# New issue orders and engine choices in both attention layers of a four-layer kernel

## The chip, the cores and the metric

The kernel runs on one core of a Trainium2 chip. The metric is the device time of one execution in microseconds (us). The core has five engines that run side by side, each taking its own instructions strictly in the order in which they were issued to it: TensorE (PE, matmuls and transposes), VectorE (DVE), ScalarE (ACT), GpSimd (POOL) and SyncE (SP, which here only issues DMAs). DMAs can be issued from SP's queue, ACT's or POOL's. An instruction waits on semaphores for the results that it needs, and whatever was issued behind it on the same engine waits with it.

## The reference, cut to what matters

A sequence of 2048 positions with 512 features goes through four layers, alternating between a convolution layer A and an attention layer B. Each adds its result to its input; the input is layer-normalised.

```python
def _A_ref(u, A_re, A_im, B_re, B_im, C_re, C_im, log_dt, Dskip):
    ...  # S4: build a 2048-tap kernel per channel, long convolution, + u * Dskip

def _B_ref(x, wqkv, wo):
    H = 32; Dh = D // H
    W, dil = 8, 2
    qkv = (x @ wqkv).reshape(B, S, 3, H, Dh) ...
    idx = pos[:, None] - (jnp.arange(W) * dil)[None, :]
    mask = idx >= 0
    ...
    logits = jnp.einsum("bhsd,bhswd->bhsw", q, kg) * scale
    logits = jnp.where(mask, logits, -1e9)
    attn = _softmax(logits, axis=-1)
    o = jnp.einsum("bhsw,bhswd->bhsd", attn, vg)
    return o.reshape(B, S, D) @ wo
```

So in an attention layer every position of each of the 32 heads (16 features each) looks at itself and at seven earlier positions, two apart.

## The kernel before, in words

**Stages.** The convolution kernel and the first convolution fill the span to about 160 us, attention 1 runs to about 272, convolution 2 (`a_layer`) to about 320, attention 2 to the end. `b_layer` (L1253) builds both attention layers. X holds the residual stream in bf16, 16 column blocks j of 128 positions each; position p*16+j lies on partition p, so that "two positions earlier" is mostly block j-2 on the same partition.

**An attention layer.** Work is named by fp (head group of 16 heads, 0 or 1) and jh (half of the 16 blocks).

- *Turned input.* X is transposed in four quarters q and two feature halves cp into U (XT in the code), by a transposing DMA from SP (L1307) or by eight PE transposes into pt_x (L1301) and a copy by ACT or DVE (L1304).
- *Statistics* for the normalisation: `BATCH_NORM_STATS2` on DVE in halves of 256 features (L1359) or whole (L199), aggregates (L1363), then logarithm and exponential on ACT (L1374, L1375), which give rs. The products of two rs per tap make RR (L1406 on DVE, spread by ACT at L1386, first rows set by POOL).
- *Queries and keys.* Four 128x512 matmuls make a tile ps_qk; `pair` (L1439, evacuated at L1444) takes two tiles in one or two PSUM tiles, `proj` (L1420, evacuated at L1425) takes one. ACT or DVE casts the tile into qT or kT. The last key columns are copied ahead of the first ("ahead", L1462) by DMA, ACT or DVE.
- *Logits.* DVE multiplies queries and shifted keys (prod, L1519, four instructions of 4096 elements for each fp and jh, or eight of 2048 for the first), PE sums over the features of a head with a block matrix (Lp, L1530), a cast LT (L1548) and a turn (pt_l, L1556) bring them to L (L1561).
- *Softmax.* DVE scales by RR (L1599), takes a tree of maxima (L1580) and subtracts (L1644), ACT takes the exponential (L1645); for one group PE subtracts (L1654) and ACT reads PSUM (L1658). The sum is taken on PE (ps_den, L1636) with logarithm and exponential on ACT, or by a tree and a reciprocal on DVE (L1611). DVE multiplies by it (L1664).
- *Values.* PE makes ps_v (L1474), ACT scales it into VX (L1485); SP's DMAs shift parts of VX by one partition (L1498). DVE multiplies values and weights (prod, L1695), PE sums the eight taps with an identity into po (L1711; L1716 in the form with small matmuls that needs no turn afterwards), ACT casts po to ot (L1729) or straight to oT (L1731); ot is turned by a DMA (L1734) or by PE and ACT (L1741, L1744). The last four blocks of head group 1 go in two small pieces, 12 and 14.
- *Output.* PE multiplies oT by wo into ps_o (L1795). X is then updated in one of four ways: the PE adds X itself first (L1792) and ACT casts back (L1905, L1907); DVE adds (L1767); ACT takes the result (L1773) and DVE adds it (L1776); or ACT takes it and a DMA from POOL adds it to X in memory (L1779).
- *After it.* Attention 1 normalises the new X into U for convolution 2 (squares L1913, norms on ACT L1917 or DVE L228); attention 2 stores X to the output (L1942) from SP's or ACT's queue.

**Buffers.** The products (prod) share a ring of four buffers; PSUM has two tiles psA, two psO and one psL. A tile is handed on when its last reader is done.

**What sets the order.** Nothing is scheduled at run time. `Plan` (L314) numbers the operations as they are built. Where an operation can be done in several ways, `either` builds all of them and each has numbers of its own. `run` (L340) then goes through the stage's string of numbers in `ORDERS` (L247) and issues those operations in that order; a way whose numbers aren't in the string is dropped. So a string fixes both the order on each engine's queue and the engine of each choice. The microseconds in the code (`pl.op("A", 0.71, ...)`) aren't used by `run`.

```python
        order = [int(i) for i in ORDERS[Plan.turn].split()]
        Plan.turn += 1
        taken = {self.ops[i][2] for i in order}
        ...
        for i in order:
            fn, after, way = self.ops[i]
            assert done.issuperset(after)
            fn()
            done.add(i)
```

There are four strings: the first convolution, attention 1, convolution 2, attention 2.

Of the kernel before, what the change touches and what calls it, by code (L numbers as in the profile page):

```python
# [230 lines left out]
def load_params(nc, pp, prm):  # L231
# [16 lines left out]
    "164 1 162 236 3 7 8 9 2 5 19 24 20 166 10 12 13 21 11 22 34 14 25 35 30 31 26 28 55 47 45 48 168 56 59 38 42 39 57 62 "  # L248
    "60 43 233 71 65 235 69 66 49 160 72 75 232 81 83 84 87 76 234 229 91 89 73 95 365 323 92 101 85 368 107 103 327 369 "
    "108 96 328 158 174 176 170 370 104 113 329 93 117 371 330 184 172 186 115 180 331 326 116 238 125 105 372 131 127 182 "  # L250
    "373 128 367 178 144 332 341 139 242 188 137 119 245 244 249 382 342 141 140 239 343 189 143 120 344 191 151 190 129 "
    "192 383 246 152 193 194 345 384 346 195 243 149 333 385 202 334 196 132 206 374 216 250 251 230 252 335 375 336 376 "
    "377 200 337 222 268 378 262 338 379 339 380 277 267 198 263 226 208 269 347 340 348 349 351 386 387 270 275 381 388 "
    "264 353 214 278 483 354 356 274 484 204 279 389 237 390 392 394 395 530 240 225 210 221 284 241 358 276 219 213 282 "
    "529 532 533 359 487 285 280 546 283 281 314 397 361 489 488 485 286 534 315 318 535 536 304 486 547 319 537 362 548 "
    "296 297 538 527 399 402 549 490 539 300 550 400 403 291 292 540 509 541 301 302 405 406 309 519 520 310 322 551 542 "
    "409 410 407 408 411 552 412 543 421 514 515 414 523 440 553 544 415 418 554 429 545 294 555 556 419 560 441 442 561 "
    "491 445 446 524 426 321 443 444 558 563 469 427 453 428 571 572 576 577 711 714 665 669 447 574 579 666 671 672 670 "
    "713 565 568 667 566 434 500 668 715 716 496 569 435 581 582 454 455 728 505 584 585 717 311 718 506 719 729 709 720 "
    "470 461 420 721 471 673 497 730 587 588 722 731 593 594 589 498 590 723 591 734 724 592 462 463 596 597 691 507 678 "  # L260
    "679 619 480 481 696 604 697 600 601 725 735 612 613 616 605 847 851 726 732 617 727 853 733 736 737 738 742 848 743 "
    "516 740 854 892 627 643 436 849 850 895 910 602 700 618 852 896 624 698 625 897 898 753 754 899 900 746 608 609 682 "
    "901 902 756 477 747 911 912 913 914 882 478 628 903 915 748 904 905 906 758 759 629 761 705 750 763 706 644 751 764 "
    "958 907 635 766 767 645 626 908 909 525 651 610 887 769 775 888 770 776 771 772 773 774 873 878 652 879 916 960 975 "
    "778 779 917 653 976 977 978 979 891 636 687 782 637 918 922 961 962 963 964 965 688 923 783 785 790 980 680 920 809 "
    "966 925 981 791 659 660 801 967 793 662 689 817 927 792 930 928 931 810 663 811 968 969 933 934 798 939 940 799 937 "
    "938 970 971 818 819 935 972 973 864 806 807 869 936 974 982 708 870 784 833 983 987 988 986 990 855 860 861 825 941 "
    "834 949 992 995 994 808 997 840 826 830 831 998 999 1000 890 872 800 863 1001 946 947 1002 1003 948 1004 841 1005 "
    "1009 1014 1010 1022 842 954 955 1011 881 1012 1038 844 1023 845 1019 956 1013 1030 1039 1020 1040 1025 1046 1031 1047 "
    "1037 1026 1048 1063 1064 1054 1060 1061 1057 1021 1055 1058",  # L270
    "127 169 126 168 40 170 83 172 175 145 173 146 136 132 102 262 304 305 84 128 171 263 264 93 214 259 103 46 260 261 "
    "215 85 7 216 131 273 325 326 44 86 50 43 190 87 253 13 196 197 198 0 235 236 237 56 129 1 199 39 200 201 191 82 192 "
    "45 254 255 174 176 316 317 2 322 283 238 239 89 125 88 90 91 42 41 47 222 130 133 177 392 240 393 394 395 284 398 399 "
    "396 48 134 178 179 323 397 402 406 181 229 230 182 403 231 400 401 407 404 405 408 285 298 299 313 314 307 295 296 "
    "292 293 331 332 289 290 410 411 412 183 424 416 417 352 353 286 287 413 319 320 418 419 414 415 346 420 334 347 343 "
    "344 425 426 427 428 340 358 480 341 359 349 350 381 382 484 485 429 422 423 486 355 356 482 430 481 459 460 461 462 "
# [26 lines left out]
    "843 853 580 581 572 573 806 813 570 587 571 595 588 589 590 601 596 786 597 602 598 584 586 593 776 854 594 599 600 "  # L303
    "591 729 592 603 811 917 809 730 735 925 731 732 741 742 926 918 919 739 844 740 939 733 734 831 736 743 744 927 737 "
    "738 883 884 920 745 746 893 894 863 747 864 940 941 953 954 955 873 874 857 969 859 861 807 907 967 909 904 971 974 "
    "905",
]


# [1668 lines left out]
```

## Time and profile before

| what | value |
|---|---|
| time, median of 3 runs | 430.04 us (429.09 to 430.61) |
| span of the profiled execution | 429.5 us |
| PE busy | 379.0 us |
| VectorE busy | 402.9 us |
| ScalarE busy | 321.2 us |
| GpSimd busy | 27.7 us |

The profile is of one execution, whose span is 0.5 us under the median of the runs. Rows of its timeline read: start, duration, engine, line, operation, output and inputs with their shapes, how many in a row, and in brackets how long the engine had stood idle before and what ended that. Durations of single PE instructions contain their latency, so that rows of several overlap. A row of a window table gives for a stretch of time the busy time of each engine, then the granted PE clock as a share of full speed, and the DMA engines' load.

### The profile page before, as it was taken

The page shows a single profiled execution, that of the slowest core. Times are in us where ns is not written, and L with a number is a line of the kernel's source. Part 1 is how long each engine was busy: PE and PEld are TensorE (multiplying, and loading weights), DVE is VectorE, ACT ScalarE, POOL GpSimd, SP SyncE. Part 2 cuts the span into 40 slices and gives each one's busy share as a digit, 9 for nine tenths or more (in the row PEclk, how much of TensorE's full clock was granted, in tenths as well). Part 3 has the DMA queues.
Part 4 walks back from the last instruction along what each step waited for, and adds up shares of the span by engine and source line. Part 5 has one row for each costly group of instructions (what it writes and reads, how often), then busy time and mean ns, then how long its engine had stood idle before and what let it go on. Part 6 is the DMA issues. An engine that isn't in the chain of part 4 may idle for free.

```text
span 429.5 us, 11615 instructions
## 1 busy us (share of the span) xinstructions
PE 379.0 (88%) x4834; PEld 235.4 (55%) x4834; DVE 402.9 (94%) x682; ACT 321.2 (75%) x524; POOL 27.7 (6%) x97
## 2 busy tenths in 40 slices
PE   2269868997998889999997899899999999998996
PEld 1153646776877764347643345577864336743452
DVE  6999999899999789999899989999889899999995
ACT  7999999999998664668752478999956578853341
POOL 1000000000000200000000510020000010000150
PEclk9757989999999999999999799999999999999999
DMA  8997067688977774012222597099973000222297
GB/s 231 201 294 292 37 87 150 150 161 173 187 123 140 143 173 102 0 38 60 77 55 56 123 209 159 14 178 191 188 121 28 37 2 2 86 85 56 44 154 189
DMA packets 102203, 51.49 MB, mean 120 GB/s; under 512 B 81851, under 2 KB 94028, under 8 KB 101894
## 3 DMA queue, kind: packets, MB, share of 16 engines
q1 hardware_dynamic: 98214, 44.98, 48.9%
q0 software_dynamic: 3104, 5.24, 6.4%
q8 instruction: 38, 0.62, 0.6%
q10 hardware_dynamic: 832, 0.52, 0.4%
q14 instruction: 15, 0.12, 0.1%
HBM read 19.30 MB, written 6.29 MB: 60 GB/s over the span
## 4 chain that ended last, share of the span: by engine, by line
PE 46%; DVE 23%; ACT 9%; issue 4%; DMA 1%; DVEq 0%; ACTq 0%
PE po L1711 8%; PE ps_v L1474 7%; PE ps_qk L1420 6%; PE ps_qk L1439 6%; DVE prod L1695 4%; PE ps_o L1795 4%; PE Lp L1530 4%; DVE pa L967 3%; DVE Tscr L474 3%; DVE prod L1519 2%; DVE Ytab L480 2%; ACT xc L1162 2%; PE vp L1183 1%; PE ps_s L1117 1%; DVE Ytab L467 1%
## 5 line engine op out<-in xcount | busy, mean ns | idle before, releaser
L1695 DVE TENSOR_TENSOR prod<-VX,L 128x512 bf16<-128x512 bf16 (+2 forms) x72 | 75.7, 1102 | 2.2 <-ACT VX L1485 1.0
L1519 DVE TENSOR_TENSOR prod<-qT,kT 128x4096 bf16<-128x4096 bf16 (+1 forms) x40 | 72.1, 1862 | 2.1 <-ACT kT L1462 1.0
L1711 PE MATMUL po<-prod,sb_ident 128*128 128x512 bf16 x240 | 57.1, 380 | 2.3 <-DVE prod L1695 2.0
L1711 PEld LDWEIGHTS <-sb_ident 128*128 128x128 bf16 x240 | 23.2, 98 | 31.5 <-issue 4.4
L1795 PE MATMUL ps_o<-wo_t,oT 128*128 128x512 bf16 x128 | 33.1, 387 | 0.2 <-ACT oT L1744 0.2
L875 ACT CAST Z<-ps_s 128x1024 bf16<-128x1024 f32 (+1 forms) x36 | 32.0, 933 | 1.3 <-PE ps_s L872 1.2
L1474 PE MATMUL ps_v<-wv,U 128*128 128x256 bf16 x256 | 31.4, 273 | 0.6 <-ACT VX L1485 0.3
L1729 ACT CAST ot<-po 128x1024 bf16<-128x1024 f32 (+1 forms) x16 | 15.1, 958 | 22.2 <-PE po L1711 22.2
L1420 PE MATMUL ps_qk<-U,wqk 128*128 128x512 bf16 x128 | 30.6, 380 | 0.3 <-ACT L L1658 0.3
L1485 ACT ACTIVATE VX<-ps_v,rs 128x256 bf16<-128x256 f32 x64 | 26.7, 473 | 5.6 <-PE ps_v L1474 5.1
L1439 PE MATMUL ps_qk<-U,wqk 128*128 128x512 bf16 x128 | 29.3, 379 | 0.0
L1474 PEld LDWEIGHTS <-U 128*128 128x128 bf16 x256 | 24.3, 98 | 8.9 <-issue 3.1
L1530 PE MATMUL Lp<-prod,sb_bones 128*32 128x512 bf16 x256 | 23.7, 398 | 2.5 <-DVE prod L1519 2.4
L892 PE MATMUL xp<-zt,sb_C 128*128 128x512 bf16 x64 | 19.4, 387 | 3.8 <-ACT zt L912 2.1
L1359 DVE BATCH_NORM_STATS2 pst<-X 128x6 f32<-128x256 bf16 x64 | 22.0, 414 | 0.5 <-ACT X L1209 0.5
L1420 PEld LDWEIGHTS <-wqk 128*128 128x128 bf16 x128 | 11.8, 98 | 16.8 <-issue 3.6
L967 DVE TENSOR_TENSOR pa<-sp_u,sp_k 128x2048 bf16<-128x2048 bf16 x16 | 19.4, 1222 | 1.5 <-ACT sp_k L903 1.2
L1795 PEld LDWEIGHTS <-oT 128*128 128x128 bf16 x128 | 12.4, 99 | 15.2 <-issue 1.0
L1439 PEld LDWEIGHTS <-wqk 128*128 128x128 bf16 x128 | 12.2, 98 | 15.4 <-issue 1.6
L1171 DVE TENSOR_TENSOR pa<-xc,Kt 128x2048 bf16<-128x2048 bf16 x16 | 19.0, 1222 | 1.2 <-DMA Kt<-kt_scratch 0.8
L872 PE MATMUL ps_s<-KT,FK 128*128 128x128 bf16 (+1 forms) x360 | 18.8, 209 | 1.0 <-ACT KT L845 0.5
L872 PEld LDWEIGHTS <-FK 128*128 128x128 bf16 x360 | 17.4, 98 | 3.2 <-issue 2.3
(230 smaller groups left out, 848.1 us busy)
## 6 DMA issues: line engine op xcount, KB each, us to landing
kt_scratch<-sp_k SPq DMA_DIRECT2D x16, 256.0 KB, 3.1
Kt<-kt_scratch POOLq DMA_DIRECT2D x16, 256.0 KB, 6.7
sp_u<-sp_u SPq DMA_DIRECT2D x18, 128.0 KB, 3.1
X<-in_A_u_dram SPq DMA_DIRECT2D x8, 256.0 KB, 5.9
X<-in_A_u_dram SPq DMA_DIRECT2D x4, 512.0 KB, 5.2
Kt<-kt_scratch SPq DMA_DIRECT2D x8, 256.0 KB, 4.9
VX<-VX SPq DMA_DIRECT2D x4, 448.0 KB, 3.7
out_dram<-X SPq DMA_DIRECT2D x14, 128.0 KB, 2.9
```

The lines of the kernel that those rows point to most:

```text
L872: nc.tensor.matmul(ps[:, r, 0:n // 4, jj * 4:(jj + 1) * 4], w, x, start=(k == 0), stop=(k == len(todo) - 1))
L875: nc.scalar.copy(box["Z", kind, dc, b0][:, 0:n // 4, :, jq * 16:(jq + 1) * 16].rearrange("p g r k -> p r g k"), box.pop(("s1", kind, dc, j ...
L967: nc.vector.tensor_tensor(pr[:], box["U"][:, s:t + 1:t - s], k[:].unsqueeze(1).to_broadcast([128, 2, 1024]), ALU.mult)
L1420: nc.tensor.matmul(ps[:], wqk[:, ct, f0:f0 + 128], XT[:, ct // 2, 4 * s:4 * s + 4, ct % 2, :], start=(ct == 0), stop=(ct == 3))
L1439: nc.tensor.matmul(box[name][:, k * 512:k * 512 + 512], wqk[:, ct, f0:f0 + 128], XT[:, ct // 2, 4 * s:4 * s + 4, ct % 2, :], start=(ct == ...
L1474: nc.tensor.matmul(ps[:, jj].rearrange("p t h d -> p (t h d)"), XT[:, ct // 2, j + jj, ct % 2, :], wv[:, ct, fp * 256:(fp + 1) * 256], sta ...
L1485: nc.scalar.activation(out, ps, ACT.Identity, scale=r)
L1519: nc.vector.tensor_tensor(pr[:], windows(q, 0, 2), windows(kT[fp][:, a:a + n2, col(w):col(w) + 1024], -DIL * 128, 2), ALU.mult)
L1530: nc.tensor.matmul(Lp[r0:r0 + 32, w // 4, :], bones[:, w % 4 + k, :], pr[:, k, f2 - a, hb * 512:(hb + 1) * 512], start=(n == 1 and k == 0) ...
L1695: nc.vector.tensor_tensor(p2[:].rearrange("p w j t d h -> p w (j t) d h"), windows(v, -DIL * 256, taps), l.to_broadcast([128, taps, nj * 2 ...
L1711: nc.tensor.matmul(po[:, c:c + 512], ident[:], p2[:, t, k + j:k + j + 2].rearrange("p j t d h -> p (j t d h)"), start=first, stop=stop)
L1795: nc.tensor.matmul(ps, oT[:, ft // 2, o:o + 128], wo_t[:, ft, :], start=(ft == 0 and not res), stop=(ft == 3))
```

## The change

Two of the four strings in `ORDERS` are replaced, those of attention 1 and attention 2; those of the two convolutions hold the same numbers, wrapped otherwise. No other line of the kernel is touched. The beginnings of the two strings:

```diff
-    "127 169 126 168 40 170 83 172 175 145 173 146 136 132 102 262 304 305 84 128 171 263 264 93 214 259 103 46 260 261 "
-    "215 85 7 216 131 273 325 326 44 86 50 43 190 87 253 13 196 197 198 0 235 236 237 56 129 1 199 39 200 201 191 82 192 "
...
+    "136 82 171 169 85 262 175 45 88 128 44 83 126 127 170 39 50 143 144 174 7 196 190 131 263 264 93 214 304 305 99 215 "
+    "216 1 325 326 13 197 198 221 41 89 56 130 84 172 87 86 241 191 192 199 200 201 322 242 259 260 261 43 90 168 42 173 "
...
-    "122 162 34 79 164 33 10 165 78 1 241 36 123 167 11 44 35 196 178 125 130 179 242 87 208 243 80 180 229 230 231 136 "
-    "325 40 181 50 182 183 326 81 77 197 198 119 120 38 93 209 244 82 210 215 126 245 246 121 259 268 76 269 270 232 233 "
...
+    "77 122 130 119 33 121 148 1 87 44 78 151 150 126 8 36 82 34 81 136 190 125 37 208 9 35 241 242 83 93 184 120 191 "
+    "243 209 210 244 50 185 192 245 39 193 194 149 186 259 274 40 79 152 76 214 80 246 38 123 195 386 392 388 325 260 "
...
```

Read through `Plan`, the strings say this.

**Attention 1, engine choices.** The turned input of quarter 2, cp 1, goes by DMA and that of quarter 3, cp 1, by PE with a copy on ACT; both were PE with a copy on DVE. The key ends of head group 0 go by ACT (first feature tile) and by DMA (second); both were on DVE. One key pair takes one double PSUM tile and one ACT cast of 1024 in place of two of 512; one query pair takes two PSUM tiles and two ACT casts in place of one cast of 1024 on DVE. The norms of blocks 1, 3, 6 and 7 move from DVE to ACT. Of the output tiles, 10 and 15 pass from PE and ACT to a DVE addition, 11 and 13 the other way.

**Attention 1, order.** The input's transposes and the first query and key tiles come in another sequence. In the second softmax part of head group 0 the exponential is issued earlier. The value products of (1,0) run in the sequence 4, 2, 0, 6 of the taps on DVE, while PE sums them as 0, 2, 4, 6. The first output tile (5) stands on PE ahead of the turned logits of (1,1), and the casts, squares and norms of the first output quarters stand earlier on ACT.

**Attention 2, engine choices.** The turned input of quarter 0, cp 1, is copied by ACT in place of DVE. The statistics of quarter 3 take four whole instructions (L199) in place of eight halves. Three pairs swap between one double cast and two single ones. Key ends: (0,0) and (1,0) go from ACT to DMA, (0,1) from DMA to DVE. One key cast of 512 goes from ACT to DVE. Piece 14 takes the small-matmul form without a turn. Output 2 goes from a DVE addition, and output 5 from ACT with a DVE addition, to ACT with an accumulating DMA from POOL, so that there are eight of these; output 13 goes from a DVE addition out of PSUM to ACT with a DVE addition. The stores of blocks 0, 1, 3, 4, 5, 6, 7, 11, 12 and 14 move from SP's queue to ACT's, those of 8 and 15 from ACT's to SP's.

**Attention 2, order.** Five of the statistics instructions stand between the first eight products in place of before them. Outputs 0 and 4 stand on PE before the third and fourth value sum of (0,8). Output 15 is last in place of 9. On ACT's queue the store of block 0 stands behind the take of output 4 and before the takes of outputs 7 and 3 and the casts of the value sums (0,8); it waits for the accumulating DMA of output 0. The stores of blocks 3, 7, 6 and 4 stand likewise between the later casts of pieces 12 and 14.

109 rows, old and new, of the table ORDERS are left out of this document.

## The prediction, on record before the changed kernel was run

> **What bounds the kernel now.** First the page's busy shares and the chain that ended last.
>
> ```profile
> PE 379.0 (88%) x4834; PEld 235.4 (55%) x4834; DVE 402.9 (94%) x682; ACT 321.2 (75%) x524; POOL 27.7 (6%) x97
> PE 46%; DVE 23%; ACT 9%; issue 4%; DMA 1%; DVEq 0%; ACTq 0%
> ```
>
> VectorE is busy for 94% of the span, yet the chain runs twice as long through TensorE. Only the attention layers are laid anew, so stages decide: attention 1 lies at about 160 to 272 us, attention 2 at 320 to 429.5. The windows of 10 us show which engine is full in each.
>
> ```profile
> core 0: us, PE busy (x) PEld busy (x) DVE busy (x) ACT busy (x) POOL busy (x), PEclk, DMA share, GB/s
> 160.00:170.00 10.00, 9.68 (x57) 4.91 (x57) 8.10 (x27) 4.01 (x7) 0.00 (x0) 1.00 0.49 113
> 230.00:240.00 10.00, 6.70 (x57) 2.85 (x55) 9.97 (x6) 4.90 (x7) 0.00 (x0) 0.75 0.14 26
> 260.00:270.00 10.00, 10.00 (x58) 4.70 (x56) 9.96 (x29) 8.91 (x24) 0.00 (x0) 1.00 0.60 133
> 390.00:400.00 10.00, 8.47 (x43) 3.72 (x42) 9.90 (x6) 2.91 (x4) 0.31 (x3) 1.00 0.38 74
> 410.00:420.00 10.00, 10.00 (x69) 5.31 (x68) 9.64 (x24) 3.24 (x5) 4.71 (x4) 1.00 1.03 152
> ```
>
> DVE sets the pace through the middle of both layers; at both ends PE is full too. At 230 PE waits while DVE is full, and its granted clock drops. Finer windows and PE's timeline there:
>
> ```profile
> 230.00:232.00 2.00, 1.40 (x11) 0.54 (x12) 2.00 (x2) 0.62 (x1) 0.00 (x0) 1.00 0.00 0
> 232.00:234.00 2.00, 0.56 (x8) 0.16 (x8) 2.00 (x1) 1.35 (x2) 0.00 (x0) 1.00 0.19 38
> 234.00:236.00 2.00, 1.85 (x24) 0.89 (x24) 2.00 (x2) 0.43 (x2) 0.00 (x0) 0.76 0.49 93
> 236.00:238.00 2.00, 1.39 (x12) 0.14 (x7) 1.97 (x3) 0.71 (x2) 0.00 (x0) 0.50 0.00 0
> 240.00:242.00 2.00, 2.00 (x6) 0.70 (x5) 2.00 (x2) 0.94 (x3) 1.29 (x5) 0.53 0.68 131
> ```
> ```profile
> 231.94 0.62 PE L1530 MATMUL Lp<-prod,sb_bones 128*32 128x512 bf16 x8 [0.60 <-DVE prod L1519]
> 234.15 0.61 PE L1530 MATMUL Lp<-prod,sb_bones 128*32 128x512 bf16 x8 [1.59 <-DVE prod L1519]
> 238.51 1.03 PE L1556 MATMUL pt_l<-sb_ident,LT 128*128 128x128 bf16 x8 [1.11 <-ACT LT L1548]
> ```
>
> The clock is halved from about 235.5 to 241 us: 5.5 us that do 2.75 us of work. From 238.5 on PE runs without a gap of note to the end of the layer, so all of it is paid there.
>
> **The change part by part: attention 1.** These are DVE's rows at the points where I set the two orders side by side.
>
> ```profile
> 161.02 0.69 DVE L1304 COPY U<-pt_x 128x1024 bf16<-128x1024 bf16 x1 [1.50 <-ACT X L1007]
> 165.48 0.36 DVE L1462 COPY kT<-kT 128x768 bf16<-128x768 bf16 x1 [0.88 <-ACT kT L1444]
> 172.81 6.91 DVE L1519 TENSOR_TENSOR prod<-qT,kT 128x2048 bf16<-128x2048 bf16 x6 [0.55 <-ACT kT L1444]
> 182.11 1.22 DVE L1444 CAST qT<-ps_qk 128x1024 bf16<-128x1024 f32 x1
> 207.41 4.49 DVE L1695 TENSOR_TENSOR prod<-VX,L 128x4096 bf16<-128x4096 bf16 x2 [1.00 <-ACT VX L1485]
> 249.08 0.42 DVE L1580 TENSOR_TENSOR sm<-L 128x512 bf16<-128x512 bf16 x1 [0.78 <-ACT L L1645]
> 251.97 5.14 DVE L1695 TENSOR_TENSOR prod<-VX,L 128x1024 bf16<-128x1024 bf16 x8
> 261.72 0.41 DVE L228 TENSOR_SCALAR U<-X,ln_rstd_a,ln_nb_a 128x512 bf16<-128x512 bf16 x1
> ```
>
> Off DVE go two copies of transposed input (2 x 0.69), two copies of key ends (2 x 0.36), one query cast (1.22) and four norms (4 x 0.41): 5.0 us. The out tiles that swap ways cancel. The start: the last X cast on ACT still ends at 160.3, whichever order follows. By then DVE has statistics to do on columns that are complete, in place of the wait of 1.50; with the copies gone and the casts for the first product ordered earlier, I walk the first product to 170.2, a lead of 2.6. Some of it is lost again: the spread of RR stands on ACT behind a row of casts, and its user on DVE waits some 1.2 us. The missing cast and the missing wait of 1.00 give it back: 3.1 of lead at the product now at 207.41. A wait of about 1.1 for the second softmax takes it to some 2.0. At 249.08 the wait of 0.78 for the exponential is gone, and the lead at 251.97 is 2.8; behind it lie the four norms, so DVE would end the layer 4.0 to 4.3 us early.
>
> One turned input now goes through SP's transposing DMA, and so do key ends; on SP the three cp 1 transposes stand with the loads of bones and wo.
>
> ```profile
> U<-X SPq DMA_TRANSPOSE x13, 3.3
> X<-oT POOLq DMA_DIRECT2D x6, 128.0 KB, 4.6
> L1779 POOL DMA_DIRECT2D X<-oT x6: 1178/1442/2136, 406.1 to 415.5; - x6
> out_dram<-X SPq DMA_DIRECT2D x14, 128.0 KB, 2.9
> L1942 ACTq DMA_DIRECT2D out_dram<-X x2: 396/402/408, 424.4 to 425.7; - x2
> ```
>
> The last one issues at about 162.4 and lands 3.3 later, at 165.7, where PE asks for it at 166.4 to 167.7. Cover 0.7; if a load gets ahead of it the first casts slip by that much, 0 to 1.3 us (one issue of 1.3 more). I take 0.
>
> PE: the third product of value group (1,0) is asked for first, so PE idles about 1.6 us at 222, and at 231 to 234.4 it waits 0.8 and 1.3 us for products, about what it waits now. So I keep the half-clock stretch in my forecast. What is better: the first out projection (1.07 us) now stands ahead of the turned logits and fills that wait. PE then stands about 3.5 us ahead of today at the same work.
>
> ACT is what bounds the gain at the layer's end.
>
> ```profile
> 252.02 1.01 ACT L1729 CAST ot<-po 128x1024 bf16<-128x1024 f32 x1 [2.27 <-PE po L1711]
> 271.75 1.05 ACT L1907 CAST X<-ps_o 128x512 bf16<-128x512 f32 x2
> 274.36 1.93 ACT L1121 CAST Z<-ps_s 128x1024 bf16<-128x1024 f32 x2
> L1917 ACT ACTIVATE U<-X,ln_nb_a,ln_rstd_a 128x512 bf16<-128x512 bf16 x6 | 4.7, 808 | 0.2 <-DVE ln_nb_a L221 0.2
> ```
>
> From 252.02 to 274.36 ACT has hardly a gap; then come the first casts of conv 2, in which ACT is again the full engine. Four norms at 0.81 add 3.2 us to that stretch. Were nothing else moved, 2.8 of lead minus 3.2 would leave a loss of 0.4. Against it stands that ACT is half idle from 220 to 250 (4.90 of 10 in one window) and the new order puts the casts and squares of quarters 0 and 1 there. Walked through, ACT is free for conv 2 at 270.3, not 274.36: 4.1 us. Bounds: -0.4 and +4.1. A walk leaves out the small waits that every row above has, and of three such points in this layer (0.55, 1.00, 0.78) I expect one or two to come back elsewhere. I take +2.8, nearer the walk, since DVE's lead at 251.97 is that much on its own.
>
> **Conv 2** is issued as before and moves along with it.
>
> **Attention 2.** The waits in its start and the rows of its end:
>
> ```profile
> 330.26 4.64 DVE L1519 TENSOR_TENSOR prod<-qT,kT 128x2048 bf16<-128x2048 bf16 x4 [1.00 <-ACT kT L1462]
> 335.37 4.64 DVE L1519 TENSOR_TENSOR prod<-qT,kT 128x2048 bf16<-128x2048 bf16 x4 [0.47 <-ACT nm L1374]
> 340.70 1.23 DVE L1548 CAST LT<-Lp 128x1024 bf16<-128x1024 f32 x1 [0.70 <-PE Lp L1530]
> ```
> ```profile
> 414.55 2.42 PE L1716 MATMUL po<-sb_ident,prod 128*128 128x128 bf16 x32
> 421.56 0.39 PE L1741 MATMUL pt_o<-sb_ident,ot 128*128 128x128 bf16 x4
> 421.78 4.05 PE L1795 MATMUL ps_o<-wo_t,oT 128*128 128x512 bf16 x18
> 425.87 0.69 DVE L1767 TENSOR_TENSOR X<-ps_o,X 128x512 bf16<-128x512 f32 x1 [0.17 <-PE ps_o L1795]
> ```
>
> The first product can start at 328.4, 1.9 early, since the turned input is copied by ACT and the key ends go by DMA. But five statistics steps that today stand ahead of it now stand between the products, with a cast and a copy that were not on DVE: the cast of Lp at 340.70 gets only 0.7 earlier. From there to 400 DVE is full in both orders and keeps that lead. The tail is PE's: in 410 to 420 it has no gap, and it is solid to the 421.78 row's end. There DVE's savings (two additions to X fewer, at most 0.69 each, and one shorter) lie beside PE's work and are worth nothing; should PE gain a gap there, they would be worth their 1.4 us. Piece 14 without the flat form takes 32 small matmuls (2.42) for 8 wide (8 x 4.05/18 = 1.80) and, counted or not, four transposes (0.39): +0.2 to +0.6 on PE, its full engine. In return two out projections go ahead of the last value sums, into the gaps that make 390 to 400 only 8.47 full. Net, walked: the last addition 0.3 us early.
>
> The stores: ten go to ACT's queue at 0.40 each, and some stand there ahead of casts. Store 0 is queued behind its own accumulating DMA, issued about 401 and landing 4.6 later, near 405.7; ACT comes to it at 403.8, and the casts of out 7, out 3 and the value sums behind it wait for 2 us. PE, with two psA buffers, runs on out 7 and the sums until 406.5 and loses 0.4, which is in the 0.3 above. Stores 3, 7, 6 and 4 come 2 to 15 us after their landing: no wait. Bounds for this layer: +0.7 (no wait at all) and -2.3 (0.3 less a whole wait of 2 and the 0.6 of piece 14). I take +0.3.
>
> [...]
>
> **The sum.** 429.5 (span of the profiled execution) - 2.8 - 0.3 = 426.4. The median of the runs is 430.04, 0.54 above the span, so 426.9.
>
> **The rivals.**
> (a) The half clock goes. It falls after waits of 0.60 and 1.59 us with 0.56 of 2 us busy; new waits of 0.8 and 1.3 may just miss that. Then up to 2.75 us of PE work comes back, half of it useful before ACT binds: 426.9 - 1.4 = 425.5. For: little would do. Against: the wait moves, but hardly shrinks. [...]
> (b) ACT's tail eats the lead in attention 1: the four norms (3.2) at 252 to 274 stay on the path, and only 0.3 to 0.5 remain: 429.6. For: ACT's 8.91 of 10. Against: its idle half from 220 to 250.
> (c) A second half-clock stretch, after the new wait of 1.6 at 222, costs 2.75 more: 429.6. Against: PE is otherwise full in those 4 us.
> (d) Slower: ACT's queue stands before the stores. If POOL's accumulating DMAs, in one queue, are late by one issue each (1.4), stores 0, 3 and 7 each hold ACT for 2 us or more, behind them the evacuations that PE's two psA buffers wait for, in the stretch where PE is the bound; 3 x 2 = 6 us less 0.4 of slack, with the layer 1 gain kept: 426.9 + 5.6 = 432.5. It decides from a hold of about 1.4 us per store on. For: no store stands ahead of ACT's work today, so nothing shows it. Against: stores 3 and 7 have long slack in my walk.
>
> **How the numbers follow.** My forecast 0.50, (a) 0.12, (b) 0.15, (c) 0.08, (d) 0.15. The range leaves out a tenth on each side: 424.0 (walk in full, 430.04 - 4.1 - 0.7 = 425.2, and half clock gone) to 431.8 (most of (d)). The bound is 0.3%, 1.3 us, about what a measurement of this kernel can tell from no change: faster under 428.7, slower over 431.3. Faster: nearly all of my case and (a), a tenth of (b) and (c): 0.63. Same: (b), (c), what spills over from mine: 0.20. Slower: (d) and a remainder: 0.17.
>
> **What would show it.** Right: first product of attention 1 near 170, the product now at 207.41 near 204.3, conv 2's first cast near 271; in attention 2 the first product 1.9 early against conv 2's end and the last addition nearly level. Wrong: an ACT row of a cast that waits for a DMA near 404; a clock under 1.00 elsewhere than about 232 to 241; DVE standing for more than 2 us in the first 30 us of attention 1.

## The result and the profile after

| | before | after |
|---|---|---|
| time, median of 20 runs each | 429.38 us (428.01 to 430.81) | 427.88 us (426.33 to 430.53) |
| ratio after to before, 95% interval | | 0.9966 (0.9951 to 0.9981) |
| span of the profiled execution | 429.5 us | 426.5 us |

The change makes the kernel 1.5 us faster; the interval times 429.4 us gives 0.8 to 2.1. The first two lines of the page of after, busy shares and chain:

```profile
PE 367.5 (86%) x4808; PEld 234.7 (55%) x4846; DVE 396.9 (93%) x668; ACT 326.0 (76%) x529; POOL 30.1 (7%) x99
PE 14%; DVE 5%; issue 2%; ACT 2%; DMA 2%; POOL 0%; DVEq 0%; ACTq 0%
```

DVE has 6.0 us less to do and ACT 4.8 more. PE's 11.5 us less can't be read as work: part of it is clock (a mean of 0.964 in this profile of before, 0.974 in that of after), and 38 matmul records are missing (x4808 beside 4846 weight loads). The chain covers only a quarter of the span here, so the stages decide again. Lines of after stand one lower than those of before (L1518 is before's L1519), those of the experiments that are shown stand between one lower and four higher. Windows of after, at the places where the prediction showed those of before:

```profile
160.00:170.00 10.00, 10.00 (x54) 4.71 (x53) 8.78 (x33) 6.40 (x9) 0.00 (x0) 1.00 0.41 79
230.00:240.00 10.00, 8.00 (x70) 3.58 (x69) 9.97 (x7) 6.08 (x12) 1.70 (x6) 1.00 0.28 56
232.00:234.00 2.00, 1.05 (x16) 0.47 (x17) 2.00 (x2) 1.35 (x3) 0.00 (x0) 1.00 0.43 85
234.00:236.00 2.00, 1.19 (x11) 0.46 (x12) 1.97 (x3) 0.58 (x1) 0.00 (x0) 1.00 0.94 177
260.00:270.00 10.00, 8.86 (x63) 4.73 (x63) 9.85 (x31) 9.64 (x22) 0.00 (x0) 1.00 0.47 107
410.00:420.00 10.00, 9.00 (x89) 5.89 (x88) 6.51 (x17) 3.85 (x6) 2.39 (x2) 1.00 1.04 157
```

The clock stays at 1.00 from 230 to 240. ACT is now nearly full at the end of attention 1 (9.64, before 8.91), and in 410 to 420, where PE had no gap before, it has gaps of 1.0 us in all. The rows that bound the stages of after: the last cast of conv 1 to X, the first cast of conv 2 to Z, conv 2's last cast, attention 2's first product, the last addition to X.

```profile
157.91 1.56 ACT L1006 CAST X<-ps_y 128x512 bf16<-128x512 f32 x3 [0.74 <-PE ps_y L1002]
...
269.79 2.40 ACT L1120 CAST Z<-ps_s 128x1024 bf16<-128x1024 f32 x3
...
314.57 1.99 ACT L1208 CAST X<-ps_y 128x1024 bf16<-128x1024 f32 x3 [0.31 <-PE ps_y L1203]
...
325.00 2.36 DVE L1518 TENSOR_TENSOR prod<-qT,kT 128x2048 bf16<-128x2048 bf16 x2 [2.10 <-ACT qT L1443]
...
422.50 0.69 DVE L1766 TENSOR_TENSOR X<-ps_o,X 128x512 bf16<-128x512 f32 x1 [0.17 <-PE ps_o L1794]
```

Attention 1 is counted from the end of conv 1's last cast (157.91 + 1.56 = 159.47) to the start of the first Z cast: 269.79 - 159.47 = 110.3. The same subtractions for the profiles of the experiments below (two much slower ones left out; "the end" is the end of the span):

| profile | attention 1 | conv 2 | attention 2 to the last addition | from there to the end |
|---|---|---|---|---|
| before | 114.1 | 45.4 | 106.9 | 2.9 |
| a2_only (old attention 1) | 114.0 | 44.7 | 106.5 | 2.9 |
| before_fill, before_fill2 | 112.3, 112.3 | 44.7, 44.7 | 106.9, 107.1 | 2.9, 2.9 |
| a1_only, a1_again (new attention 1, old attention 2) | 110.9, 110.8 | 45.7, 44.7 | 106.5, 106.5 | 2.7, 2.8 |
| a1_late_out | 111.2 | 44.7 | 106.5 | 2.8 |
| after, after_again | 110.3, 111.1 | 46.8, 44.7 | 106.6, 106.8 | 3.3, 3.3 |
| norms_dve | 111.8 | 44.8 | 107.0 | 3.3 |
| after_no_pool, after_late_adds | 111.2, 110.7 | 46.9, 44.7 | 107.2, 106.9 | 3.9, 3.4 |

### The profile page after: what moved, and what is told of

It is laid out like the page before. It is cut to its first block, busy times and chain, and to the rows that moved or that the text cites. A ratio compares the mean times of both kernels' runs of the same rounds, so it can differ in the third digit from the quotient of the medians.

```text
span 426.5 us, 11606 instructions
## 1 busy us (share of the span) xinstructions
PE 367.5 (86%) x4808; PEld 234.7 (55%) x4846; DVE 396.9 (93%) x668; ACT 326.0 (76%) x529; POOL 30.1 (7%) x99
## 5 line engine op out<-in xcount | busy, mean ns | idle before, releaser
L1518 DVE TENSOR_TENSOR prod<-qT,kT 128x4096 bf16<-128x4096 bf16 (+1 forms) x40 | 72.4, 1858 | 4.5 <-ACT qT L1443 3.3
L1710 PE MATMUL po<-prod,sb_ident 128*128 128x512 bf16 x225 | 53.5, 379 | 1.8 <-DVE prod L1694 1.3
L1794 PE MATMUL ps_o<-wo_t,oT 128*128 128x512 bf16 x123 | 31.0, 379 | 1.2 <-DMA oT<-ot 0.9
L1728 ACT CAST ot<-po 128x1024 bf16<-128x1024 f32 (+1 forms) x15 | 14.2, 984 | 20.3 <-PE po L1710 20.3
L1529 PE MATMUL Lp<-prod,sb_bones 128*32 128x512 bf16 x256 | 19.8, 382 | 2.6 <-DVE prod L1518 2.6
L1358 DVE BATCH_NORM_STATS2 pst<-X 128x6 f32<-128x256 bf16 x56 | 19.3, 408 | 1.9 <-ACT X L1006 1.8
L891 PE MATMUL xp<-zt,sb_C 128*128 128x512 bf16 x45 | 15.0, 380 | 5.1 <-ACT zt L911 2.3
```

The lines of the kernel that those rows point to most:

```text
L1518: nc.vector.tensor_tensor(pr[:], windows(q, 0, 2), windows(kT[fp][:, a:a + n2, col(w):col(w) + 1024], -DIL * 128, 2), ALU.mult)
L1529: nc.tensor.matmul(Lp[r0:r0 + 32, w // 4, :], bones[:, w % 4 + k, :], pr[:, k, f2 - a, hb * 512:(hb + 1) * 512], start=(n == 1 and k == 0) ...
L1710: nc.tensor.matmul(po[:, c:c + 512], ident[:], p2[:, t, k + j:k + j + 2].rearrange("p j t d h -> p (j t d h)"), start=first, stop=stop)
L1794: nc.tensor.matmul(ps, oT[:, ft // 2, o:o + 128], wo_t[:, ft, :], start=(ft == 0 and not res), stop=(ft == 3))
```

## The experiments

**One layer at a time.** a1_only (run a second time as a1_again) takes one of the two new strings, a2_only the other.

```diff
 ORDERS = [
-    attention 1: the string of before
+    attention 1: the string of after      (a1_only, a1_again)
-    attention 2: the string of before
+    attention 2: the string of after      (a2_only)
 ]
```

> The kernel before with the order of attention 1 alone from after. Theory 'attention 1 earns it': the first cast of conv 2 stands 3.8 us nearer to the last X cast of conv 1 than before, as in after, and the median is 1.5 to 2.8 us under before, so at least all of what after gains (1.5). Rival 'attention 2 has a share of its own': the gain here is under 1 us. Second question, conv 2: if its longer span in after (46.8 us from first to last cast, before 45.4) comes from the new order ahead of it, it is over 46 here too; if it was an accident of one execution, it is near 45.4 and the gain nearer 2.8.

> The kernel before with the order of attention 2 alone from after. Theory: 0.2 to 0.5 us under before, not to be told from none; first product 2 us earlier against conv 2's end, last addition to X nearly level. Rival 'the stores and the two more accumulating DMAs cost': 0.5 to 1.5 us over before. Rival 'attention 2 carries the gain': 1.5 us under.

> The kernel before with the order of attention 1 alone from after, once more, on one chip with after. Theory 'attention 2's new order earns nothing and its stores cost some tenths at the end': 0 to 0.8 us under after. Rival 'attention 2 gives 0.3 to 0.5': 0.3 to 0.5 over after.

> The kernel after, unchanged, for a second profile and to stand beside the others on one chip. Theory: clock 1.00 through all of attention 1 again, 110.3 us (within 0.6) from the last X cast of conv 1 to the first Z cast of conv 2 (before 114.1); conv 2 back near 44.7 to 45.4, since the 46.8 of the first profile came from transfers that were late in that execution; attention 2 with its last addition 106.5 to 106.9 after conv 2's end, as before. Rival 'the earlier end of attention 1 makes conv 2's transfers collide': 46 or more again in conv 2. Median 427 to 428.

| kernel | median, runs | ratio to before, 95% interval |
|---|---|---|
| a1_only | 427.07 us, 6 | 0.9941 (0.9918 to 0.9965) |
| a1_again | 427.77 us, 8 | 0.9948 (0.9927 to 0.9970) |
| a2_only | 429.23 us, 12 | 0.9986 (0.9968 to 1.0004) |
| after_again | 428.03 us, 12 | 0.9968 (0.9950 to 0.9986) |

Attention 1's string alone earns all of it: 2.2 to 2.5 us by the ratios, where after has 1.4 to 1.5. Attention 2's string alone can't be told from no change. The new attention 1 with the old attention 2 is so the best version by its median, though its intervals overlap those of after.

The two strings don't simply add up. From conv 2's end to the end of the span the table has, on average, 109.8 us for the old attention 2 behind the old attention 1 (before and the two fills), 109.3 for the new one behind the old attention 1 (one profile), 109.3 for the old one behind the new attention 1, and 110.1 where both are new (after, after_again, norms_dve). In the third case 0.35 us comes from one wait. Behind the old attention 1, DVE waits 0.47 us for `nm` from ACT ahead of its fifth product (before's row at 335.37 in the prediction). Behind the new one the same string runs all eight products through, though ACT's rows stand at the same places:

```profile
326.75 9.39 DVE L1519 TENSOR_TENSOR prod<-qT,kT 128x2048 bf16<-128x2048 bf16 x8 [1.00 <-ACT kT L1462]
```

This row is a1_again's. Why the wait goes isn't known, but a part of what a1_only gains so lies outside attention 1. Against that, the device time of the 24 runs of a1_only, a1_again and a1_late_out is 1.8 to 3.0 us longer than their spans, 2.1 on average, where it is 1.7 to 1.9 in the runs of before beside them and in all runs of after: some 0.3 us of the gain go again behind the last instruction that the table counts.

In the table of stages conv 2 takes 44.7 or 44.8 us wherever none of its transfers is late, under old and new orders alike; the 45.4, 45.7, 46.8 and 46.9 are single executions. In the profile of after:

```profile
291.11 2.36 DVE L1170 TENSOR_TENSOR pa<-xc,Kt 128x2048 bf16<-128x2048 bf16 x2 [0.56 <-DMA Kt<-kt_scratch]
...
291.88 0.39 PE L1157 MATMUL xp<-zt,sb_C 128*128 128x512 bf16 x1 [1.34 <-DMA zt<-Z]
```

Both wait for a transfer; in after_again, the same kernel, conv 2 is back at 44.7. So this is not a price of the new order.

**TensorE's clock.** before_fill leaves before's order as it is and gives PE work to do in the two waits of 0.60 and 1.59 us that the prediction showed; before_fill2 adds transposes in the wait of 1.11 behind them. What they write is overwritten by the real work.

```diff
+                    if center and (fp, jh) == (1, 1):          # both kernels, ahead of the sums into Lp
+                        for x in range({2: 3, 4: 7}.get(w, 0)):
+                            nc.tensor.matmul(Lp[:, w // 4, :], ident[:], kT[0][:, 0, 0:512], start=True, stop=True,
+                                             skip_group_check=True)
...
+                if center and (fp, jh) == (1, 1):              # before_fill2 alone, ahead of the turn into pt
+                    for x in range(18):
+                        nc.tensor.transpose(pt[:, x % 2, :, x // 2 % 4, :], ident[:], ident[:])
```

> The kernel before, order unchanged, with 3 and 7 matmuls of 128x512 more on TensorE in the two waits of 0.60 and 1.59 us ahead of the logit sums at 231.9 and 234.2 (their output is overwritten). Theory 'the half clock there is what the new order gets rid of': the clock is 1.00 through 230 to 242, the 2.75 us of work lost there come back in part, and the first cast of conv 2 comes 1.3 to 2.7 us earlier; median 1 to 2 us under before. Rival 'ACT's tail bounds the layer's end whatever TensorE does': clock 1.00, yet conv 2's first cast moves by under 0.5 and the median by under 0.4. Rival 'the drop of the clock has nothing to do with these waits': the clock still drops.

> The kernel before with the 3 and 7 matmuls of before_fill in the waits of 0.60 and 1.59 us, and 18 transposes of 128x128 more in the wait of 1.11 for the cast of those logits, their output overwritten. Theory 'the dips of TensorE's work between 231 and 239 are what halves its clock there': share of runs with a mean clock of 0.99 to 0.997 or under 0.97 falls from two thirds to the third that the kernels with the new attention 1 show, 112.3 us from conv 1's end to conv 2's start, median 0.4 to 1 us under before. Rival 'it is chance or the state of the chip': the share stays at two thirds.

Windows of before_fill where before had its half clock, and its first Z cast:

```profile
232.00:234.00 2.00, 2.00 (x19) 0.74 (x15) 2.00 (x2) 0.83 (x1) 0.00 (x0) 1.00 0.47 92
234.00:236.00 2.00, 1.51 (x28) 0.79 (x24) 2.00 (x2) 0.59 (x2) 0.00 (x0) 1.00 0.21 40
236.00:238.00 2.00, 0.89 (x16) 0.44 (x9) 1.97 (x2) 1.50 (x2) 0.00 (x0) 1.00 0.00 0
```
```profile
272.07 3.90 ACT L1121 CAST Z<-ps_s 128x1024 bf16<-128x1024 f32 x5
```

In before_fill's profile the clock is full throughout (a mean of 1.00) and the layer takes 112.3 us, as it does in before_fill2's; in the two profiles with the old order and nothing filled in, the clock halves (windows of 0.50 in before and in a2_only) and the layer takes 114.1 and 114.0. So this stretch costs about 1.75 us. Yet the medians don't move: 429.54 us, ratio 0.9994 (0.9971 to 1.0017), and 429.24 us, 1.0000 (0.9986 to 1.0014). A likely reason is in the mean clock of each run, which adds up all half-clock stretches of an execution, wherever they lie. In the profile of after one half-clock stretch, of 20.5 us near the kernel's start (0.50 in every window of 2 us from 16 to 36), goes with a mean clock of 0.974; in those of a1_again and after_late_adds one of 3.4 us goes with 0.995 and 0.994; before has 20.5 us near the start and 3.4 and 6.8 us later, and 0.964. From these an estimate for the others: a mean of 0.970 to 0.972 is the stretch at the start and 3.4 us more, the 0.968 of a2_only is 6.8 us more. Runs with a mean clock under 0.97 are 33 of the 92 of before that were taken beside the experiments, with a mean of 430.4 us; 7 of 24 for the two fills (6 of 12 and 1 of 12); 13 of 92 for the eight series with the new attention 1. The fills' share can't be told from before's; what is shown is what the stretch in attention 1 costs, not that these waits bring it on.

The 17 runs of before whose clock was 0.999 or 1.000 have a mean of 428.4 us, the six such runs of after 427.5, the five of a1_only and a1_again 427.2. So 0.9 to 1.2 us of the gain is there without any half clock.

a1_late_out takes away what the prediction saw as filling PE's wait: the first output tile goes behind the turn of the last logits again, in the kernel a1_only.

```diff
 attention 1, from after:
-    PE out 5; ACT cast LT; PE turn pt_l; ACT cast of out 5; ACT cast of L
+    ACT cast LT; PE turn pt_l; PE out 5; ACT cast of L; ACT cast of out 5
```

> The kernel with attention 1 alone from after, and in it the first out projection (four matmuls and one of 128x512, 1.1 us) put behind the turn of the last logits instead of ahead of it, so that TensorE has nothing to do in the wait for the cast of those logits. Theory 'that filling is what keeps the clock up': the clock falls to 0.50 near 235 to 241 in some executions, 1.75 us lost in these, and the share of runs with a mean clock of 0.99 to 0.997 or under 0.97 rises to about the two thirds that before has; median 0.7 to 1.8 over a1. Rival 'the filling is worth only its own 1.1 us, the clock has to do with the waits ahead': conv 2's start 0 to 0.5 later, share of such runs as low as in a1.

428.10 us (10 runs), ratio 0.9964 (0.9945 to 0.9984); attention 1 takes 111.2, 0.3 to 0.4 more than in a1_only. Its windows:

```profile
234.00:236.00 2.00, 0.85 (x20) 0.33 (x12) 2.00 (x2) 0.42 (x2) 0.00 (x0) 1.00 0.89 170
236.00:238.00 2.00, 0.89 (x16) 0.45 (x9) 1.97 (x2) 1.01 (x1) 0.00 (x0) 1.00 0.49 92
```

PE is busy for less than half of these four microseconds (1.74), and the clock stays full in this execution. Two of ten runs had a mean clock under 0.97, none of 14 of a1_only and a1_again: too few to tell. The four profiles with the filling and the new attention 2 (after, after_again, after_no_pool, after_late_adds) spread from 110.3 to 111.2, so the 0.3 to 0.4 us are no more than the spread. Neither a worth of the filling nor that it keeps the clock up is shown.

**Choices and places.** The new string for attention 1 changes engines and moves instructions. choices_only takes the engines and leaves the places, places_only takes the places and leaves the engines. The remaining choices, the casts of one key pair and the output tiles 10, 11, 13 and 15, stay with the places in both.

```diff
 choices_only: the string of before for attention 1, with
-    DVE: two copies U<-pt_x, two copies of key ends, one cast of qT, norms 1, 3, 6, 7
+    DMA and ACT: one U each; ACT and DMA: key ends; ACT: two casts of qT, norms 1, 3, 6, 7
 places_only: the string of after for attention 1, with the same lines the other way round
```

> The kernel before with the engine choices of attention 1 that take work off DVE (one turned input to DMA and one to ACT, one copy of key ends to ACT and one to DMA, one query cast and four norms to ACT), each at the place that its instruction had in the old order; nothing else is moved. Theory 'the choices earn it': the start of conv 2 comes 1.4 us or more earlier than before at full clock (112.3 from conv 1's end), median 1 us or more under before. Rival 'it is the places': the casts and norms wait at their old places in ACT's queue and lengthen its tail by 4 x 0.81 less 4 x 0.41 = 1.6 us, so 0 to 2 us over before.

> The kernel with attention 1 alone from after, but with the engine choices of before for two turned inputs, two copies of key ends, one query cast and four norms (all back on DVE, 2 x 0.69 + 2 x 0.36 + 1.22 + 4 x 0.41 = 5.0 us of DVE's time) at the places of the new order. Theory of the prediction 'the 5.0 us off DVE are the gain': first product 1.5 to 2.5 us later than in a1, start of conv 2 113.5 to 115 us after conv 1's end (a1 110.8), no gain left over before. Rival 'the places alone earn it': under 112.3, a median under before.

choices_only: 438.28 us, ratio 1.0198 (1.0174 to 1.0223). places_only: 436.18 us, 1.0167 (1.0144 to 1.0190). Each half alone is 7 to 9 us slower than before. In choices_only, read upwards: DVE's first product waits for a copy of key ends on ACT, that stands behind casts which wait for PE, and PE waits for the turned input that now comes by DMA and was issued at the old, late place.

```profile
168.94 5.77 PE L1440 MATMUL ps_qk<-U,wqk 128*128 128x512 bf16 x26 [2.45 <-DMA U<-X]
...
171.29 0.59 ACT L1445 CAST qT<-ps_qk 128x512 bf16<-128x512 f32 x1 [4.56 <-PE ps_qk L1440]
...
176.64 0.82 ACT L1463 COPY kT<-kT 128x768 bf16<-128x768 bf16 x1
...
177.49 3.50 DVE L1520 TENSOR_TENSOR prod<-qT,kT 128x2048 bf16<-128x2048 bf16 x3 [10.11 <-ACT kT L1463]
```

In places_only DVE itself stands before the copies of key ends, whose casts aren't done at the early place:

```profile
168.31 0.36 DVE L1462 COPY kT<-kT 128x768 bf16<-128x768 bf16 x1 [4.02 <-ACT kT L1444]
...
174.36 0.36 DVE L1462 COPY kT<-kT 128x768 bf16<-128x768 bf16 x1 [1.80 <-ACT kT L1444]
```

Neither expectation had the size: the one reckoned with 0 to 2 us, the other with no gain left. What both miss is a chain of three in-order queues, in which a late step of 1 us of work holds up all that stands behind it: the rows of choices_only have waits of 2.45 us on PE, 4.56 on ACT and 10.11 on DVE.

norms_dve undoes one choice that hangs on nothing at the layer's start: the four norms.

```diff
-    ... 817 ... 815 ... 794 ... 790 ...      norms of blocks 7, 6, 3, 1 by ACT
+    ... 818 ... 816 ... 795 ... 791 ...      the same by DVE, at the same places
```

> The kernel after with the four norms that went to ACT (of positions 1, 3, 6 and 7) done by DVE again, each at the same place of the order. Theory of the prediction: DVE's lead there goes by 4 x 0.41 = 1.6 us, ACT's tail is 4 x 0.81 = 3.2 shorter; ACT had room in 220 to 250, so the time is the same or up to 1 us longer. Rival 'ACT's tail is what bounds the layer's end' (it is busy 9.64 of 10 in 260 to 270 after the change): conv 2's first cast comes 1 to 3 us earlier and the median falls by 0.7 or more.

429.13 us, ratio 0.9984 (0.9964 to 1.0004) against 0.9966 and 0.9968 of after: 0.7 us given back, with intervals that overlap, and attention 1 takes 111.8 in place of 110.3 and 111.1. So the rival, a gain of 0.7 or more, is out, and the theory (the same, or up to 1 us longer) fits: the norms seem better off on ACT, although ACT is 96% busy in 260 to 270. With overlapping intervals this is likely, but not certain.

**Attention 2's tail.** Every profile with the new attention 2, except after_no_pool below, has one wait in PE's full stretch that none with the old one has. Here it is in after, with SP's transposes before it and SP's last stores after it:

```profile
404.41 7.87 SPq L1733 DMA_TRANSPOSE oT<-ot  x3
...
412.90 0.60 PE L1794 MATMUL ps_o<-wo_t,oT 128*128 128x512 bf16 x2 [0.95 <-DMA oT<-ot]
...
420.19 3.46 SPq L1941 DMA_DIRECT2D out_dram<-X  x6
```

It is 0.80 in a2_only, 1.14 in after_again, 1.30 in norms_dve. The transposes' median from issue to landing between 403 and 425 us, in a1_again and in after_again:

```profile
oT<-ot SPq DMA_TRANSPOSE x3, 3.8
```
```profile
oT<-ot SPq DMA_TRANSPOSE x3, 5.8
```

The suspicion was the two more accumulating DMAs from GpSimd. after_no_pool has out 2 added by DVE from PSUM where ACT had taken it, and out 5 copied by ACT and added by DVE late; after_late_adds keeps ACT's copies and puts DVE's two additions where DVE waits for PE anyway.

```diff
-    out 2: ACT X<-ps_o copy, POOL accumulate     out 5: the same
+    after_no_pool:   out 2: DVE adds from PSUM   out 5: ACT copy, DVE adds late
+    after_late_adds: out 2: ACT copy, DVE adds late   out 5: the same
```

> The kernel after with outs 2 and 5 of attention 2 added to X by DVE again, as before (out 2 straight from PSUM, out 5 from its copy), in place of GpSimd's accumulating DMAs. Theory 'the two more accumulating DMAs crowd the transfers of the tail': TensorE's wait of 0.8 to 1.3 us for the transposed value sums (oT from ot) at 96 us after conv 2's end goes, the transposes land in 4.1 us or less instead of 4.3 to 5.8, conv 2's end to the last addition is 0.3 to 0.9 us shorter (106.0 to 106.4) and the median 0.3 to 0.9 under after. Rival 'the wait is the earlier stores' doing, or the transposes are simply asked for too early': the wait stays at 0.8 or more and the time within 0.3. Rival 'DVE needs the relief': the last addition comes 0.4 to 1.1 us later.

> The kernel after with outs 2 and 5 of attention 2 copied by ACT as in after, but added to X by DVE (0.43 each, from the copy) in place of GpSimd's accumulating DMAs, at the two places in the tail where DVE waits about 1 us for TensorE anyway; no product is held up, as it was in after_no_pool. Theory 'the two more accumulating DMAs crowd the tail's transfers': TensorE's wait of 0.8 to 1.3 us for the transposed value sums (oT from ot) shrinks under 0.5, the transposes land in about 4 us, the last addition comes 0.3 to 0.9 us earlier (106.0 to 106.4 after conv 2's end) and the median is 0.3 to 0.9 under after's. Rival 'the transposes are asked for too early in the new order, whoever adds': wait of 0.8 or more, last addition 106.5 to 107, median within 0.4 of after's.

after_no_pool: 429.58 us, ratio 0.9997 (0.9980 to 1.0015). It settles nothing: DVE's addition stood in front of products, PE waited 1.45 us for a product instead (until 414.42), and its output tile at 415.10 has no wait for the transposes. after_late_adds: 427.85 us, 0.9964 (0.9945 to 0.9982), the same as after, with the wait still there:

```profile
412.28 0.60 PE L1794 MATMUL ps_o<-wo_t,oT 128*128 128x512 bf16 x2 [1.19 <-DMA oT<-ot]
```
```profile
oT<-ot SPq DMA_TRANSPOSE x3, 5.8
```

So the two more accumulating DMAs aren't the cause, and this theory falls. The cause stays open. Two suspects are left, the place on PE of the output tile that needs the turned sums, and the new order of the stores; neither was tried alone.

## Why the prediction was right, and where it was not

Right in direction: 426.9 was forecast from a base of 430.0, so 3.1 us faster, and 1.5 were measured; the time of 427.9 lies inside the range. That the time came out nearer than the gain is partly luck: the base was the median of three runs, and over twenty runs before has 429.4, so of the 1.6 by which the gain was too large 0.7 doesn't show in the time. By its own steps:

**The start of attention 1: right.** First product at 170.2 forecast; 169.56 in after, where conv 1 ended 0.8 earlier, so 10.1 us behind it and not 9.9. The stall for RR was put at some 1.2; it is 0.83.

```profile
169.56 2.36 DVE L1518 TENSOR_TENSOR prod<-qT,kT 128x2048 bf16<-128x2048 bf16 x2 [1.23 <-ACT qT L1443]
...
178.29 2.37 DVE L1518 TENSOR_TENSOR prod<-qT,kT 128x2048 bf16<-128x2048 bf16 x2 [0.78 <-PE Lp L1529]
...
190.50 0.69 DVE L1598 TENSOR_TENSOR L<-L,RR 128x1024 bf16<-128x1024 bf16 x1 [0.83 <-POOL RR L1391]
...
202.97 0.69 DVE L1663 TENSOR_TENSOR L<-L,sm_rdb 128x1024 bf16<-128x1024 bf16 x1 [0.72 <-ACT sm_rdb L1620]
...
204.34 2.29 DVE L1694 TENSOR_TENSOR prod<-VX,L 128x4096 bf16<-128x4096 bf16 x1 [0.34 <-ACT VX L1484]
...
249.46 3.70 DVE L1694 TENSOR_TENSOR prod<-VX,L 128x1024 bf16<-128x1024 bf16 x6
```

**The step that failed: the lead of 2.8 at before's 251.97, and the 2.8 in the sum made from it.** The lead was forecast as 2.6 at the first product, 3.1 at the product at 207.41, 2.0 behind the second softmax and 2.8 at 251.97. Counted from conv 1's end and at full clock it is 2.4, 2.3, 1.1 and 0.7. These are rows of before_fill (the old order at full clock) and of a1_only, whose conv 1 ends 0.2 us earlier (159.5 against 159.8):

```profile
204.60 0.69 DVE L1648 TENSOR_TENSOR L<-L,sm_m 128x1024 bf16<-128x1024 bf16 x1
...
206.90 2.29 DVE L1699 TENSOR_TENSOR prod<-VX,L 128x4096 bf16<-128x4096 bf16 x1 [1.00 <-ACT VX L1485]
...
247.56 0.42 DVE L1584 TENSOR_TENSOR sm<-L 128x512 bf16<-128x512 bf16 x1
...
250.44 3.10 DVE L1699 TENSOR_TENSOR prod<-VX,L 128x1024 bf16<-128x1024 bf16 x5
```
```profile
204.39 2.29 DVE L1695 TENSOR_TENSOR prod<-VX,L 128x4096 bf16<-128x4096 bf16 x1 [0.34 <-ACT VX L1485]
206.60 0.28 DVE L1580 TENSOR_TENSOR sm<-sm 128x256 bf16<-128x256 bf16 x1
206.92 0.23 DVE L1580 TENSOR_TENSOR sm_m<-sm 128x128 bf16<-128x128 bf16 x1
207.18 0.69 DVE L1644 TENSOR_TENSOR L<-L,sm_m 128x1024 bf16<-128x1024 bf16 x1
...
249.52 3.70 DVE L1695 TENSOR_TENSOR prod<-VX,L 128x1024 bf16<-128x1024 bf16 x6
```

- *3.1 counted, 2.3 measured* (206.90 - 204.39 - 0.2). DVE has waits that the walk left out, in after 0.78 for Lp at 178.29 and 0.72 for sm_rdb at 202.97, and of the wait of 1.00 that was to go 0.34 is left. The forecast time of 204.3 was hit by luck: conv 1 ended 0.8 earlier in after's execution.
- *2.0 counted, 1.1 measured.* The wait of 1.1 for the second softmax isn't there. In its place two steps of the maximum and the subtraction (0.28 + 0.23 + 0.69 = 1.2), which stood ahead of the product, now stand behind it.
- *2.8 counted, 0.7 measured* (250.44 - 249.52 - 0.2). The wait of 0.78 at before's 249.08 that was to go is no part of the old order: at full clock the same instruction, before_fill's row at 247.56, has none. It came with the half-clock stretch of before's one execution, which reached the product of 251.97 91.7 us after conv 1 (251.97 - 160.27), where before_fill needs 90.7 (250.44 - 159.76).

The prediction kept the stretch in its forecast for both sides, so it meant the 2.8 as order alone. As order alone it is 0.7, and the whole layer, the norms included, gains 1.5 at full clock where 2.8 was entered.

**The four norms: right, as far as the runs can tell.** DVE's 1.6 us for them is worth 0.7 in the time, by norms_dve; with the lead of 0.7 that makes 1.4, about the 1.5 by which the layer is shorter at full clock (112.3 against 110.8, the mean of the four profiles of after and a1). Rival (b), ACT's tail, didn't happen.

**The layer as a whole.** 3.8 us shorter in the profile (114.1 to 110.3), which would look like the walk of 4.1 come true. At full clock it is 1.5; the rest is clock and the spread of 0.8 between profiles. Rival (a), to which the prediction gave 0.12, is what the profile shows: after's clock is 1.00 over 160 to 270. Of the others with the new order, a1_only has a mean clock of 0.999, a1_again 0.995, with its 3.4 us in conv 1, and a1_late_out's windows from 232 to 240 have 1.00. The second stretch of rival (c) didn't come either. The 1.4 us that (a) put on the stretch were near the 1.75 that it costs. Over many runs it weighs little: the share of runs under 0.97 falls by 20 of 92, and these are 1.1 us longer than before's runs between 0.97 and 0.99 (430.4 against 429.3), which makes 0.2 us on average.

**Conv 2 moves along: right**, though the one profile of after says otherwise by 1.4 us.

**Attention 2: the start right, the end wrong.** The first product stands 8.4 us after conv 2's end and not 10.5: 2.1 earlier, 1.9 forecast. At the end nearly nothing of that is left, as forecast for DVE: against the old order behind the old attention 1 the last addition comes 0.2 us earlier (106.6 and 106.8 us after conv 2 in after and after_again, 106.9 to 107.1 in before and the two fills), where 0.3 was forecast. But from it to the end of the span it takes 3.3 us in place of 2.9, a step that the prediction left out. So it is about +0.2 in place of -0.3. Beside it stands that eleven of the 16 stores are issued from 417.8 on, six of them from SP's queue at 420.19, as shown above, and five from ACT's; a1_again has twelve of SP's spread from 413.3 on (the second row is its own). That this is the cause wasn't tried, and one profile speaks against it: a2_only has its stores as late as after and takes 2.9.

```profile
417.81 3.37 ACTq L1941 DMA_DIRECT2D out_dram<-X  x5
```
```profile
413.31 9.79 SPq L1942 DMA_DIRECT2D out_dram<-X  x12
```

The wait of PE for a transpose was in none of the steps either.

**The store on ACT: wrong, without consequence.** Store 0 was to hold ACT for 2 us until about 405.7. It was issued at 401.65. Rival (d) didn't happen.

```profile
401.65 0.41 ACTq L1941 DMA_DIRECT2D out_dram<-X  x1
```

Put together again with the measured terms: -1.5 for attention 1 at full clock, -0.2 for the clock, +0.2 for attention 2: 1.5 us faster, against 1.5 (0.8 to 2.1) measured. Each term is uncertain by some tenths, so that the sum meets the measured value to the tenth is chance.

## What to carry to other kernels

A lead read at one instruction is a lead only if the same work lies ahead of it in both orders; where work has been moved behind the instruction, subtract it. A wait that goes is a gain only if it is there at the same clock (the 0.78 at 249.08 was not). Before a sum is made against one profiled execution, look for what that execution alone has (here a half-clock stretch worth 1.75 us and late transfers worth up to 2.2) and set like against like. Changes in two stages needn't add up either: the old attention 2 ran 0.35 us shorter behind the new attention 1, by a wait that went away. Engine choices and places in in-order queues could not be priced one by one here: either half of attention 1's change costs 7 to 9 us, both together win 2.2 to 2.5.

## What the runs showed of the hardware that was not expected

The same instructions at the same place of the kernel run at half clock in one execution and at full clock in another. Windows of a1_again and of a1_only, the same kernel, in conv 1:

```profile
98.00:100.00 2.00, 0.95 (x10) 0.55 (x9) 1.97 (x2) 2.00 (x3) 0.00 (x0) 1.00 0.73 158
100.00:102.00 2.00, 1.50 (x9) 0.94 (x9) 2.00 (x2) 1.82 (x3) 0.00 (x0) 0.60 0.89 299
102.00:104.00 2.00, 2.00 (x24) 1.87 (x22) 2.00 (x3) 1.48 (x2) 0.00 (x0) 0.55 0.66 122
```
```profile
98.00:100.00 2.00, 0.79 (x9) 0.48 (x8) 1.97 (x2) 2.00 (x3) 0.00 (x0) 1.00 0.94 208
100.00:102.00 2.00, 1.52 (x18) 1.17 (x18) 2.00 (x2) 2.00 (x4) 0.00 (x0) 1.00 0.66 250
```

The execution in which PE was busier in 98 to 100 (0.95 against 0.79) is the one that falls. The length of the stretch is estimated from the rows: if the clock is either 1.00 or 0.50, as before's windows from 236 to 240 have it, a window of 2 us with a mean of 0.60 has 1.6 us at half clock and one with 0.55 has 1.8: 3.4 us. Before's stretch at 234 to 242 (0.76, 0.50, 0.50, 0.53) comes by the same working to 6.8 us, and not 5.5 as the prediction read it.

What sets the moment at which the clock falls is not shown. From 231.6 to 235.0, ahead of before's fall, PE was busy for 1.5 us and never stood for longer than 1.59 in a row; from 98 to 100, ahead of a1_again's fall at 100.4, it was busy for 0.95. In a1_late_out it was busy for less, 0.85 and 0.89 us in the two windows from 234 to 238, and the clock stayed at 1.00 there.
